# Mixers: the first half's low part of the squares directly behind the second half's mean, and no piece of the weights' conversion in slot 24

## The chip, the cores and the metric

The kernel runs on one core of one Trainium2 chip. The metric is the device time of one execution in microseconds (us), as the median of several runs. Beside it stands one profiled execution, from which all views of the trace come.

## The reference

Three layers follow one another, over 8 batches of 576 positions and 512 channels: a landmark attention, a first mixing layer with an MLP, and a second mixing layer with an MLP. The change lies in the second mixing layer, of which this is the whole:

```python
def _moe2_ref(x, w_ch1, w_ch2):
    X = np.fft.fft(x, axis=1)
    X = np.fft.fft(X, axis=2)
    mixed = np.real(X).astype(np.float32)
    u = x + mixed
    mu = np.mean(u, axis=-1, keepdims=True)
    var = np.mean((u - mu) ** 2, axis=-1, keepdims=True)
    un = (u - mu) / np.sqrt(var + 1e-06)
    ch = np.maximum(un @ w_ch1, 0.0) @ w_ch2
    return (u + ch).astype(np.float32)
```

`w_ch1` is 512 x 2048 and `w_ch2` 2048 x 512, in both MLPs. The results are wanted in single precision.

## The kernel before, in words

**Products.** Every large product is made of three TensorE (PE) matmuls of 128 x 512: each operand is split into a high part, rounded to the matmul's format, and a low part, the rest. The high part is a cast on ScalarE (ACT); the low part, original less high, is a subtraction on VectorE (DVE) or GpSimd (POOL). `split` writes both.

**The stage in question.** From about 650 to 1300 us of the span, PE works through the MLPs in slots (`Mlp.stream`). One slot is 12 matmuls: in the upward half of a chunk one of 8 tiles of hidden units (lines 241 to 243, then `relu` on ACT at line 245 and the low part `g` on DVE at line 246), in the downward half one half of an output tile (lines 294 to 296, and every second slot `xf <- ps + xf` on DVE at line 305, which is then stored by the SP queue at line 153). Three PSUM banks `ps` take turns. After its matmuls a slot runs the steps that a table has put there, and then pieces of other work.

**The mixers.** One `Mixer` per batch does the Fourier transform and the normalization, its steps spread over 31 slots by the table in `steps`. The mixers begin at slots 33, 58, 83, 108, 133, 157, 182 and 206 of the stage; I count them 0 to 7. Slot r of a mixer is r slots behind its begin, so that slots 25 to 31 of one are slots 0 to 6 of the next. The parts that matter here:

- `load` (slot 1): SP issues the transfers of the tile `U` (lines 1169 ff.), of which there is one buffer. `load_first` (slot 3) follows at lines 1178 and 1180. `fold_d` (slots 5 and 7, line 1192) is the first to read it, on DVE.
- `row_high` (slot 5, ACT), `fold_low` (slots 8 and 10, DVE, line 1212) and the transform's matmuls `over_d` (slots 10 to 14, PE, lines 75 to 77, two banks `ps_f`, freed by a `split` into `Z`, line 51).
- `sum_u(n)`, `sums_low(n)` (slots 21 to 23): for half n of the positions the channels of `U` are added (lines 1308 and 1309), cast on ACT (line 1311) and the low part is made on DVE (line 1315; `he` and `ho` for halves 0 and 1).
- `centre(n)` (slot 24 + n): two matmuls with a matrix of ones (line 1320) give the mean, high part first and low part second; DVE takes it from `U` (line 1330, into `Z`).
- `sum_sq(n)` (slot 25 + n): ACT squares (line 1335), DVE adds (lines 1308, 1309), ACT casts (line 1311). `sums_low(n)` again (slot 26 + n, line 1315; now `le` and `lo`).
- `deviation(n)` (slot 28 + n): the same two matmuls (line 1320) on the squares' sums, then the square root on ACT, POOL and DVE.
- `put(n)` (slot 26 + n): SP stores the centred half (line 1355).

**The conversion.** The weights arrive as 64-bit numbers and are converted on the way, in pieces that `Pace.step` hands out at the end of a slot: `room(s)` says how many microseconds of it a slot takes. A tile of weights is four DVE pairs and one split: the pair at lines 1444 and 1445 (called A below), the pair at 1451 and 1453 (B), the pair at 1455 and 1456 (C), and a `split` of which POOL makes the low part. After the 32 tiles, sums of blocks of weights follow (lines 1487 and 1492), each read back from memory by four transfers (line 1477).

Within an engine, and within the SP queue, instructions run in the order in which they were issued.

Of the kernel before, what the change touches and what calls it, by code (L numbers as in the profile page):

```python
# [40 lines left out]
def body(ctx: ExitStack, tc: tile.TileContext, qT, kT, vn, mU, mV, w11, w12, w21, w22,  # L41
# [719 lines left out]
    class Batch:  # L761
# [324 lines left out]
        def steps(self, after):  # L1086

            H0, H1 = slice(0, 512), slice(512, 1152)
            a, b = (2, 1) if self.b > 1 else (0, 0)
            yield from ((2 * (nm == "q") + g - a, lambda nm=nm, g=g: self.landmark(nm, g)) for nm in "kq"  # L1090
                        for g in (0, 1) if (self.b, nm) not in LANDMARKS)
            yield from ((5 - a, self.kernel), (6 - a, self.kernel_norm), (7 - a, self.kernel_t))
            if a:
                yield 6, self.norms
            yield 6, self.scores
            if not a:
                yield 8, self.norms
            yield 9 - b, self.residue
            yield from ((10 - b + i, lambda i=i: self.newton(i)) for i in range(6))
            yield from ( (8, lambda: self.query(0)), (9, lambda: self.query(1)),  # L1100
                        (9, lambda: self.query_exp(H0)), (9, self.scores_sum), (9, lambda: self.query(2)), (10, lambda: self.scores_t(0)),
                        (11, lambda: self.scores_t(1)), (11, self.scores_tail), (11, lambda: self.query_exp(H1)),
                        (11, lambda: self.query_norm(H0)), (12, self.values), (12, lambda: self.query_norm(H1)),
                        (13, lambda: self.query_t(0)), (13, self.query_tail), (14, lambda: self.query_t(1)),
                        (15, self.mixed), (16 - b, self.heads), (17 - b, self.rank))
            if self.b:
                yield 13, lambda: self.mlp.get_tail(self.b)
                yield from ((15 + k // 2, lambda k=k: self.mlp.hand_tail(self.b, k)) for k in range(4))
            yield from ((19 + g, lambda g=g, n=n: self.mix(g, n)) for g in range(2) for n in range(2))
            if after:  # L1110
                yield from ((r, lambda nm=nm: after.load(nm)) for r, nm in ((7, "k"), (10, "q"), (13, "v")))
# [10 lines left out]
    def fourier_setup(f, fc, fp):  # L1122
        q = TAB // 4
        h = fc.tile([P, TAB], F32R, name="tabh")
        l = fc.tile([P, TAB - 148], F32R, name="tabl")
        f["eps"] = fc.tile([P, 1], F32, name="eps")
        nc.gpsimd.memset(f["eps"], 1e-6)
        for i in range(4):
            c = slice(i * q, (i + 1) * q)
            st = fp.tile([P, q], F32, name="big", bufs=2)  # L1130
            nc.sync.dma_start(st, tabs[:, c])
            yield from wait(2)
            n = min(c.stop, TAB - 148) - c.start
            split(h[:, c.start:c.start + n], l[:, c.start:c.start + n], st[:, 0:n], nc.gpsimd if i % 2 else nc.vector)
            if n < q:
                nc.scalar.copy(h[:, c.start + n:c.stop], st[:, n:q])
            yield 1
        f["ones"] = fc.tile([P, P], F32R, name="ones")
        f["row"] = fc.tile([P, NF], F32R, name="row")
        st = fp.tile([P, 1152], F32, name="big", bufs=2)  # L1140
        nc.gpsimd.memset(st[:, 0:S], 0.0)
        yield from wait(2)
        nc.sync.dma_start(zero, st[0:2, 0:S])
        nc.gpsimd.tensor_copy(f["row"], st[:, 0:NF])
        nc.gpsimd.memset(st[:, S:S + P], 1.0 / DM)
        nc.gpsimd.tensor_copy(f["ones"], st[:, S:S + P])
        yield 1
        c = 0
        for nm, n, k in (("cd", 292, 1), ("sd", 292, 1), ("ct", 290, 3), ("sn", 290, 3)):
            f[nm] = [(h[:, c + j * n:c + (j + 1) * n], l[:, c + j * n:c + (j + 1) * n]) for j in range(k)]  # L1150
            c += n * k
        f["alt"] = h[:, c:c + 146]

    class Mixer:
# [205 lines left out]
        def steps(self, last):  # L1360
            e = int(last)
            yield from ((0, self.load_x), (1, self.load), (3, self.load_first), (3, self.fold_x), (4, self.sum_row), (5, self.row_high),
                        (5, lambda: self.fold_d("e")), (5, lambda: self.fold_t("e")), (6, lambda: self.fold_2("e")),
                        (6, self.fold_row), (6, self.row_low), (7, lambda: self.fold_split("e")), (7, lambda: self.fold_d("o")),
                        (8, lambda: self.fold_low("e")), (8, lambda: self.fold_t("o")),
                        (9, lambda: self.fold_2("o")), (9, lambda: self.fold_split("o")),
                        (10, lambda: self.fold_low("o")), (11, self.load_rows))
            yield from ((s, lambda nm=nm, i=i: self.over_d(nm, i)) for s, nm, i in
                        ((10, "e", 0), (11, "e", 1), (12, "e", 2), (13, "o", 0), (14, "o", 1), (14, "o", 2)))
            yield from ((15, self.top_row), (16, lambda: self.odd(0)), (17, lambda: self.even(0)),  # L1370
                        (18, lambda: self.unfold(0)), (18, lambda: self.unfold(3)), (18, lambda: self.odd(1)),
                        (19, lambda: self.even(1)), (20, lambda: self.unfold(1)), (20, lambda: self.unfold(2)),
                        (21, self.store))
            for n in range(2):
                yield from ((21 + n, lambda n=n: self.sum_u(n)), (22 + n, lambda n=n: self.sums_low(n)), (24 + n, lambda n=n: self.centre(n)),
                            (25 + n, lambda n=n: self.sum_sq(n)), (26 + n, lambda n=n: self.sums_low(n)), (28 - e + n, lambda n=n: self.deviation(n)),
                            (26 + n, lambda n=n: self.put(n)), (29 - e + n, lambda n=n: self.newton(n)),
                            (30 - 2 * e + n, lambda n=n: self.put_scale(n)))

# [2 lines left out]
    def pool(name, **k):  # L1382
        return tc.tile_pool(name=name, bufs=1, reuse_waits="tile", **k)

    def chained(gens):
        for g in gens:
            yield from g

    def some(gen, n):
        for _ in range(n):  # L1390
            next(gen, 0)
# [156 lines left out]
    with pool("mm") as mp, pool("pm", space=PSUM) as pm:  # L1548
# [91 lines left out]
        with tc.manual_schedule():  # L1640
            scales = Scales(rs)
            mlp.plan(UN, [(c, c + 1) for c in range(PLAIN, NCH - 2, 2)] + [(NCH - 1, NCH - 2)], quarters)
            with pool("cv") as cv, pool("fp") as fp, pool("fc") as fc, pool("pf", space=PSUM) as psb:
                f = {}
                slots = Slots()
                starts = (33, 58, 83, 108, 133, 157, 182, 206)
                for b, s in enumerate(starts):
                    slots.add(s, Mixer(fp, psb, f, b).steps(b + 1 == B))
                later = Pace(chained([staging_pairs(cv, (2, 3)), staging_sums(cv)]))
                gen = mlp.stream(1)  # L1650
                setup = fourier_setup(f, fc, fp)

                def room(s):
                    r = s - max((a for a in starts if a <= s), default=-99)
                    return 1.45 if r > 40 else 1.4 if r in (*range(10, 21), 23, 24) else .7 if r in (4, 9, 21, 22) else 0

                for s in range(N + 2 * PLAIN * STEPS - LEAD):
                    if s in (N, N + PLAIN * STEPS):
                        some(gen, 9)
                        gen = mlp.stream(2 + (s > N))  # L1660
                    next(gen)
                    slots.run(s)
                    next(setup, 0)
                    later.step(room(s))
                later.rest()
            assert not slots.at
            with pool("tl") as mlp.last_pool, pool("tp", space=PSUM) as mlp.last_ps:
                last = mlp.pairs(quarters, Y, scales, U2, ByChunk(y3), block, block_sums, BLOCKS[-2:])
                next(last)
                for s in range(LEAD):  # L1670
                    next(gen)
                    next(last)
                    next(last)
                some(gen, 9)
                for _ in last:
                    pass
# [83 lines left out]
```

## Time and profile before

| | us |
|---|---|
| median of 3 runs | 1779.37 |
| lowest and highest run | 1777.63, 1780.19 |
| the profiled execution | 1780.39 |
| its span, first to last instruction | 1778.6 |
| PE busy in it | 1747.8 (98%) |
| DVE busy | 1229.9 (69%) |
| ACT busy | 749.2 (42%) |
| POOL busy | 329.6 (19%) |

The granted TensorE clock is full in all 40 slices of the span (mean 0.997). Matmuls overlap: one of 512 columns is recorded with 0.39 us, while the next begins 0.23 us after it. So PE's busy share says little; what counts is where the distance between two matmuls' starts grows. The profiled execution took 1.02 us more than the median.

### The profile page before, as it was taken

How to read it: one execution, taken by the hardware profiler on the slowest of the kernel's cores; microseconds unless marked ns; L12 is line 12 of the kernel's file. 1: busy time of each engine (PE TensorE's matmuls, PEld its weight loads, DVE VectorE, ACT ScalarE, POOL GpSimd, SP SyncE). 2: the span in 40 equal slices, each digit the busy share in tenths (PEclk: the TensorE clock that was granted, in tenths of full speed). 3: DMA queues.
4: the chain of work that ended last, by engine and by line, in shares of the span. 5: the costliest groups of instructions: out<-in, count | busy, mean ns of one | idle time of the engine just before them, and what ended most of it. 6: DMA issues, size and time to landing. Idle time of an engine off the chain costs nothing.

```text
span 1778.6 us, 31053 instructions
## 1 busy us (share of the span) xinstructions
PE 1747.8 (98%) x11869; PEld 1425.3 (80%) x11869; DVE 1229.9 (69%) x2123; ACT 749.2 (42%) x1546; POOL 329.6 (19%) x314
## 2 busy tenths in 40 slices
PE   6999999999999999999999999999999999999998
PEld 4777777777788888888878888888888888888886
DVE  7887666665322977888786665557476887589786
ACT  4544443444211333334332334434256556455543
POOL 3334212221210321211211222211201100100111
PEclk9999999999999999999999999999999999999999
DMA  7555455443536764556464955687488978878974
GB/s 255 178 180 170 153 173 195 171 157 106 180 138 224 254 236 153 177 181 223 160 206 154 346 181 175 228 304 238 157 269 294 326 263 285 260 241 260 327 234 130
DMA packets 224392, 379.92 MB, mean 214 GB/s; under 512 B 29658, under 2 KB 137530, under 8 KB 224244
## 3 DMA queue, kind: packets, MB, share of 16 engines
q1 hardware_dynamic: 218772, 367.72, 61.6%
q10 hardware_dynamic: 5472, 10.23, 1.5%
q8 instruction: 93, 1.52, 0.4%
q14 instruction: 55, 0.45, 0.1%
HBM read 269.00 MB, written 108.27 MB: 212 GB/s over the span
## 4 chain that ended last, share of the span: by engine, by line
PE 87%; DVE 7%; DMA 3%; ACT 1%; issue 1%; SPq 0%; POOL 0%; POOLq 0%; DVEq 0%; ACTq 0%
PE ps L294 9%; PE ps L241 9%; PE ps L296 9%; PE ps L295 9%; PE ps L243 9%; PE ps L242 9%; PE ps L334 8%; PE ps L333 8%; PE ps L332 8%; PE ps_f L76 1%; PE ps_f L77 1%; PE ps_f L75 1%; DMA w<-d 1%; PE ps L803 1%; DMA U<-x 1%
## 5 line engine op out<-in xcount | busy, mean ns | idle before, releaser
L241 PE MATMUL ps<-x,w 128*128 128x512 f32 x768 | 305.5, 398 | 0.2 <-DVE g L246 0.2
L294 PE MATMUL ps<-g,w 128*128 128x512 f32 x768 | 304.1, 396 | 0.0
L243 PE MATMUL ps<-x,w 128*128 128x512 f32 x768 | 299.8, 390 | 0.0
L296 PE MATMUL ps<-g,w 128*128 128x512 f32 x768 | 299.7, 390 | 0.0
L242 PE MATMUL ps<-x,w 128*128 128x512 f32 x768 | 299.5, 390 | 0.0
L295 PE MATMUL ps<-g,w 128*128 128x512 f32 x768 | 299.3, 390 | 0.0
L246 DVE SCALAR_TENSOR_TENSOR g<-ps,g 128x512 fp32r<-128x512 f32 x192 | 132.5, 690 | 206.5 <-ACT g L245 206.0
L245 ACT ACTIVATE g<-ps 128x512 fp32r<-128x512 f32 x192 | 114.2, 597 | 271.3 <-PE ps L243 270.7
L294 PEld LDWEIGHTS ps<-g,w 128*128 128x128 f32 x768 | 144.3, 188 | 32.2 <-issue 3.5
L243 PEld LDWEIGHTS ps<-x,w 128*128 128x128 f32 x768 | 144.1, 188 | 31.3
L296 PEld LDWEIGHTS ps<-g,w 128*128 128x128 f32 x768 | 144.2, 188 | 31.0
L241 PEld LDWEIGHTS ps<-x,w 128*128 128x128 f32 x768 | 144.3, 188 | 30.0 <-DVE g L246 0.6
L295 PEld LDWEIGHTS ps<-g,w 128*128 128x128 f32 x768 | 144.4, 188 | 27.3
L242 PEld LDWEIGHTS ps<-x,w 128*128 128x128 f32 x768 | 144.5, 188 | 27.0
L305 DVE TENSOR_TENSOR xf<-ps,xf 128x512 f32<-128x512 f32 x88 | 60.5, 687 | 92.2 <-PE ps L296 90.1
L414 ACT COPY ps<-ps 128x512 f32<-128x512 f32 x142 | 81.7, 576 | 87.9 <-PE ps L334 81.6
L51 POOL TENSOR_TENSOR stg<-cva,stg 128x512 fp32r<-128x512 f32 x48 | 64.7, 1347 | 216.8 <-ACT stg L50 190.3
L469 POOL TENSOR_TENSOR w<-w,w 128x512 f32<-128x512 f32 x24 | 34.8, 1450 | 363.2 <-DMA w<-rs 207.4
L332 PE MATMUL ps<-xs,w 128*128 128x512 f32 x240 | 93.4, 389 | 0.0
L333 PE MATMUL ps<-xs,w 128*128 128x512 f32 x240 | 93.4, 389 | 0.0
L334 PE MATMUL ps<-xs,w 128*128 128x512 f32 x240 | 93.4, 389 | 0.0
L51 POOL TENSOR_TENSOR x<-xf,x 128x512 fp32r<-128x512 f32 (+7 forms) x48 | 60.9, 1270 | 159.1 <-ACT x L50 123.5
(410 smaller groups left out, 3406.5 us busy)
## 6 DMA issues: line engine op xcount, KB each, us to landing
w<-e SPq DMA_DIRECT2D x96, 512.0 KB
w<-d SPq DMA_DIRECT2D x144, 256.0 KB
wraw<-w SPq DMA_DIRECT2D x56, 512.0 KB
d<-stg SPq DMA_DIRECT2D x48, 512.0 KB
w<-d SPq DMA_DIRECT2D x48, 512.0 KB
y<-xf SPq DMA_DIRECT2D x64, 256.0 KB
xf<-y SPq DMA_DIRECT2D x52, 256.0 KB
u<-u1T ACTq DMA_DIRECT2D x32, 288.0 KB
```

Source lines behind the costliest of these rows:

```text
L51: (eng or nc.vector).tensor_tensor(lo, src, f32(hi), op=ALU.subtract)
L241: nc.tensor.matmul(ps, wh, xh, start=k == 0, stop=False)
L242: nc.tensor.matmul(ps, wl, xh, start=False, stop=False)
L243: nc.tensor.matmul(ps, wh, xl, start=False, stop=k == 3)
L245: nc.scalar.activation(g[:, 0, :], ps, AF.Relu)
L246: nc.vector.scalar_tensor_tensor(out=g[:, 1, :], in0=ps, scalar=0.0, in1=f32(g[:, 0, :]), op0=ALU.max, op1=ALU.subtract)
L294: nc.tensor.matmul(ps, wh, gh, start=k == m0, stop=False)
L295: nc.tensor.matmul(ps, wl, gh, start=False, stop=False)
L296: nc.tensor.matmul(ps, wh, gl, start=False, stop=k == m1 - 1)
L332: nc.tensor.matmul(ps, wh, xh, start=first and k == 0, stop=False, skip_group_check=True)
L333: nc.tensor.matmul(ps, wl, xh, start=False, stop=False, skip_group_check=True)
L334: nc.tensor.matmul(ps, wh, xl, start=False, stop=last and k == 1, skip_group_check=True)
```

## The change

Two edits. In the mixer's table, `sums_low(0)` of the squares moves from slot 26 to slot 25, behind `centre(1)` of the same slot; to get that order the four entries of `centre` and `sum_sq` are taken out of the loop and put ahead of it. `put(0)` thereby stands behind `sum_sq(1)` of its slot instead of ahead of it. In `room`, slot 24 of a mixer gets no conversion work (1.4 us before). Slot 24 exists where the next mixer begins 25 slots later, or never: in mixers 0, 1, 2, 3, 5 and 7.

```diff
@@ -1371,9 +1371,13 @@
                         (19, lambda: self.even(1)), (20, lambda: self.unfold(1)), (20, lambda: self.unfold(2)),
                         (21, self.store))
+            yield 24, lambda: self.centre(0)
+            yield 25, lambda: self.sum_sq(0)
+            yield 25, lambda: self.centre(1)
+            yield 26, lambda: self.sum_sq(1)
             for n in range(2):
-                yield from ((21 + n, lambda n=n: self.sum_u(n)), (22 + n, lambda n=n: self.sums_low(n)), (24 + n, lambda n=n: self.centre(n)),
-                            (25 + n, lambda n=n: self.sum_sq(n)), (26 + n, lambda n=n: self.sums_low(n)), (28 - e + n, lambda n=n: self.deviation(n)),
+                yield from ((21 + n, lambda n=n: self.sum_u(n)), (22 + n, lambda n=n: self.sums_low(n)),
+                            (27 if n else 25, lambda n=n: self.sums_low(n)), (28 - e + n, lambda n=n: self.deviation(n)),
                             (26 + n, lambda n=n: self.put(n)), (29 - e + n, lambda n=n: self.newton(n)),
                             (30 - 2 * e + n, lambda n=n: self.put_scale(n)))
 
@@ -1652,7 +1656,7 @@
-                    return 1.45 if r > 40 else 1.4 if r in (*range(10, 21), 23, 24) else .7 if r in (4, 9, 21, 22) else 0
+                    return 1.45 if r > 40 else 1.4 if r in (*range(10, 21), 23) else .7 if r in (4, 9, 21, 22) else 0
```

Lines of the mixer's functions keep their numbers; the conversion's are 4 higher after the change. Since the conversion hands its pieces out one behind another, leaving out a slot moves every later piece to other slots.

**DVE, mixer 0, slots 23 to 26.** In these rows `Z<-U,ps_l` is `centre`, `cc<-big` and `cc<-cc` are `sum_sq`'s adds, `le` is the low part in question, and `xf<-ps,xf` the output tile that SP stores. Before:

```order
870 L1444 TENSOR_SCALAR cva<-wraw 128x512
871 L1445 SCALAR_TENSOR_TENSOR cva<-wraw,cva 128x512
872 L305 TENSOR_TENSOR xf<-ps,xf 128x512
873 L1330 TENSOR_TENSOR Z<-U,ps_l 128x1152
874 L1451 TENSOR_SCALAR cvp<-cva 128x512
875 L1453 SCALAR_TENSOR_TENSOR cvp<-wraw,cvp 128x512
876 L51 TENSOR_TENSOR x<-xf,x 128x512
877 L1308 TENSOR_TENSOR cc<-big 128x2x288
878 L1309 TENSOR_TENSOR cc<-cc 128x288
879 L1330 TENSOR_TENSOR Z<-U,ps_l 128x1152
880 L305 TENSOR_TENSOR xf<-ps,xf 128x512
881 L1315 TENSOR_TENSOR le<-cc,le 128x288
```

Now, at the same place:

```order
870 L1448 TENSOR_SCALAR cva<-wraw 128x512
871 L1449 SCALAR_TENSOR_TENSOR cva<-wraw,cva 128x512
872 L305 TENSOR_TENSOR xf<-ps,xf 128x512
873 L1330 TENSOR_TENSOR Z<-U,ps_l 128x1152
874 L51 TENSOR_TENSOR x<-xf,x 128x512
875 L1308 TENSOR_TENSOR cc<-big 128x2x288
876 L1309 TENSOR_TENSOR cc<-cc 128x288
877 L1330 TENSOR_TENSOR Z<-U,ps_l 128x1152
878 L1315 TENSOR_TENSOR le<-cc,le 128x288
879 L305 TENSOR_TENSOR xf<-ps,xf 128x512
```

Pair B of slot 24 is gone from here, pair A of slot 23 stays, and `le` and the output tile have changed places.

**DVE, mixer 2, slots 23 to 26.** Before:

```order
1074 L1451 TENSOR_SCALAR cvp<-cva 128x512
1075 L1453 SCALAR_TENSOR_TENSOR cvp<-wraw,cvp 128x512
1076 L1455 TENSOR_TENSOR cvp<-cvp,cva 128x512
1077 L1456 SCALAR_TENSOR_TENSOR cva<-wraw,cvp 128x512
1078 L305 TENSOR_TENSOR xf<-ps,xf 128x512
1079 L1330 TENSOR_TENSOR Z<-U,ps_l 128x1152
1080 L1444 TENSOR_SCALAR cva<-wraw 128x512
1081 L1445 SCALAR_TENSOR_TENSOR cva<-wraw,cva 128x512
1082 L1308 TENSOR_TENSOR cc<-big 128x2x288
1083 L1309 TENSOR_TENSOR cc<-cc 128x288
1084 L1330 TENSOR_TENSOR Z<-U,ps_l 128x1152
1085 L305 TENSOR_TENSOR xf<-ps,xf 128x512
```

Now, behind the same `ho` as the rows above:

```order
1070 L1459 TENSOR_TENSOR cvp<-cvp,cva 128x512
1071 L1460 SCALAR_TENSOR_TENSOR cva<-wraw,cvp 128x512
1072 L305 TENSOR_TENSOR xf<-ps,xf 128x512
1073 L1330 TENSOR_TENSOR Z<-U,ps_l 128x1152
1074 L1308 TENSOR_TENSOR cc<-big 128x2x288
1075 L1309 TENSOR_TENSOR cc<-cc 128x288
1076 L1330 TENSOR_TENSOR Z<-U,ps_l 128x1152
1077 L1315 TENSOR_TENSOR le<-cc,le 128x288
1078 L305 TENSOR_TENSOR xf<-ps,xf 128x512
```

Pair A is gone; pair B has moved to a place ahead of `ho`; `le` is ahead of the output tile.

**DVE, mixer 3, slots 9 to 11.** `Z<-ps_f,Z` frees a bank of the transform. Before:

```order
1112 L1451 TENSOR_SCALAR cvp<-cva 128x512
1113 L1453 SCALAR_TENSOR_TENSOR cvp<-wraw,cvp 128x512
1114 L246 SCALAR_TENSOR_TENSOR g<-ps,g 128x512
1115 L1212 TENSOR_TENSOR lo<-cc,ho 128x578
1116 L51 TENSOR_TENSOR Z<-ps_f,Z 97x2x144
1117 L1455 TENSOR_TENSOR cvp<-cvp,cva 128x512
```

Now:

```order
1106 L246 SCALAR_TENSOR_TENSOR g<-ps,g 128x512
1107 L1212 TENSOR_TENSOR lo<-cc,ho 128x578
1108 L51 TENSOR_TENSOR Z<-ps_f,Z 97x2x144
1109 L1455 TENSOR_SCALAR cvp<-cva 128x512
1110 L1457 SCALAR_TENSOR_TENSOR cvp<-wraw,cvp 128x512
1111 L1459 TENSOR_TENSOR cvp<-cvp,cva 128x512
```

Pair B has moved from ahead of `g` to behind the first `Z`, so that it stands ahead of all later `Z` of this mixer.

## Rows read from the trace of the kernel before

**Rows 1.** Waits of PE over the span: us in total, times, longest us.

```profile
PE ps_l L1320 <- DVE le L1315: 2.5, 2, 1.4
```

**Rows 2.** Timeline of PE, `deviation` of mixer 0: start, duration, what [idle before <- releaser].

```profile
749.77 0.29 PE L1320 MATMUL ps_l<-le,ones 128*128 128x288 f32 x1
751.44 0.40 PE L1320 MATMUL ps_l<-le,ones 128*128 128x288 f32 x1 [1.37 <-DVE le L1315]
...
754.41 0.43 PE L1320 MATMUL ps_l<-lo,ones 128*128 128x288 f32 x2
```

**Rows 3.** Timeline of DVE, mixer 0, slots 23 to 26.

```profile
740.83 1.52 DVE L1444 TENSOR_SCALAR cva<-wraw 128x512 uint32<-128x512 uint32 x1
...
745.83 0.41 DVE L1451 TENSOR_SCALAR cvp<-cva 128x512 uint32<-128x512 uint32 x1
746.27 0.69 DVE L1453 SCALAR_TENSOR_TENSOR cvp<-wraw,cvp 128x512 f32<-128x512 uint32 x1
...
747.49 0.75 DVE L1308 TENSOR_TENSOR cc<-big 128x576 f32<-128x576 f32 x1
...
748.65 1.35 DVE L1330 TENSOR_TENSOR Z<-U,ps_l 128x1152 f32<-128x1152 f32 x1
749.91 0.69 DVE L305 TENSOR_TENSOR xf<-ps,xf 128x512 f32<-128x512 f32 x1
750.51 0.87 DVE L1315 TENSOR_TENSOR le<-cc,le 128x288 fp32r<-128x288 f32 x1
```

**Rows 4.** Timeline of ACT, the same place.

```profile
745.94 1.17 ACT L1335 ACTIVATE big<-Z 128x1152 f32<-128x1152 f32 x1 [0.68 <-DVE Z L1330]
...
749.11 0.61 ACT L50 CAST x<-xf 128x512 fp32r<-128x512 f32 x1
```

**Rows 5.** Timeline of POOL, the same place.

```profile
740.71 1.34 POOL L51 TENSOR_TENSOR stg<-cva,stg 128x512 fp32r<-128x512 f32 x1 [8.66 <-ACT stg L50]
...
749.80 1.27 POOL L51 TENSOR_TENSOR x<-xf,x 128x512 fp32r<-128x512 f32 x1 [6.31 <-ACT x L50]
```

**Rows 6.** Timeline of the SP queue, the same place.

```profile
750.63 0.82 SPq L153 DMA_DIRECT2D x<-xf  x2
...
751.98 1.69 SPq L1169 DMA_DIRECT2D U<-x  x2
```

**Rows 7.** Timelines of DVE and PE, mixer 1, slots 6 to 10.

```profile
761.98 1.36 DVE L1192 TENSOR_TENSOR big<-U 128x1152 f32<-128x1152 f32 x1 [0.99 <-DMA U<-x]
...
767.44 0.69 DVE L246 SCALAR_TENSOR_TENSOR g<-ps,g 128x512 fp32r<-128x512 f32 x1 [1.12 <-ACT g L245]
...
768.31 0.40 PE L241 MATMUL ps<-x,w 128*128 128x512 f32 x1
```

**Rows 8.** Timelines of DVE and PE, from mixer 2's slot 21 to mixer 3's slot 10.

```profile
889.67 0.68 DVE L1455 TENSOR_TENSOR cvp<-cvp,cva 128x512 f32<-128x512 f32 x1
...
898.81 0.69 DVE L51 TENSOR_TENSOR x<-xf,x 128x512 fp32r<-128x512 f32 x1 [1.02 <-ACT x L50]
...
910.07 0.40 PE L1320 MATMUL ps_l<-le,ones 128*128 128x288 f32 x1 [1.13 <-DVE le L1315]
...
921.07 1.36 DVE L1192 TENSOR_TENSOR big<-U 128x1152 f32<-128x1152 f32 x1 [2.76 <-DMA U<-x]
...
927.28 0.50 PE L241 MATMUL ps<-x,w 128*128 128x512 f32 x1 [0.16 <-DVE g L246]
```

**Rows 9.** Timelines of DVE and PE, slot 14 of mixers 3 and 4.

```profile
943.39 0.44 DVE L51 TENSOR_TENSOR Z<-ps_f,Z 97x288 fp32r<-97x288 f32 x1
...
944.04 0.25 PE L75 MATMUL ps_f<-tabl,ho 128*96 128x146 f32 x1
...
1024.05 0.69 DVE L1487 TENSOR_TENSOR wraw<-cva,cvp 128x512 f32<-128x512 f32 x1 [3.26 <-DMA cvp<-d]
...
1026.48 0.36 PE L1267 MATMUL ps_f<-tabh,Z 97*33 97x290 f32 x1 [0.36 <-DVE Z L51]
```

**Rows 10.** One line's instructions, the block sums' reads: duration ns min/median/max, first and last start.

```profile
L1487 DVE TENSOR_TENSOR blk<-cva,cvp x6: 668/678/1180, 994.5 to 1259.5; 128x512 f32<-128x512 f32 x6
```

## The prediction

> **What bounds the kernel now.** I read the waits of PE first, since PE is the engine that is never out of work [rows 1]: over the whole span it waits 2.5 us for `le`, in two places. Then I looked up both places on PE's timeline. In mixer 0, `deviation(0)` begins at 749.77, and its second matmul, the low part's, would follow 0.13 us later (the pair at 754.41 takes 0.43, one matmul alone 0.29 or 0.30). It starts at 751.44 instead [rows 2]: 1.54 us lost, of which the idle entry shows 1.37, since the end of the matmul before covers the rest. In mixer 2 the same matmul starts at 910.07 behind an idle entry of 1.13 [rows 8], so 1.29 lost. The other six mixers show no such wait. Everywhere else in this stage PE begins a matmul every 0.23 us, except for 0.4 us at 927.28 (an idle entry of 0.16, the start 0.55 behind the one before, and the next 0.1 late) and 0.5 us at 1026.48 [rows 8, 9]. So all that this change can give back by PE alone is 1.54 + 1.29 = 2.8 us, and with the two small waits 3.7. About 0.2%, or 3.6 us, is what a measurement of this kernel can tell from no change.
>
> **Edit 1 and edit 2 in mixer 0.** DVE comes to `le` late because it is behind: pair A of slot 23 took 1.52 us for its first half alone [rows 3] while POOL ran [rows 5]. That pair stays. What goes is pair B, 0.41 + 0.69 = 1.1 us, and `le` passes the output tile, 0.6 us (749.91 to 750.51) [rows 3]. Taken alone that is 1.7 us, more than the 1.54 of the wait. But two things behind it are late next.
>
> First, the adds of `sum_sq(0)` cannot start before ACT's square ends, 745.94 + 1.17 = 747.11 [rows 4]; they started at 747.49 [rows 3]. So removing B brings the chain forward by 0.34 us only: adds at 747.15, `centre(1)` at 748.31, `le` at 749.57.
>
> Second, POOL makes a low part `x` from 749.80 for 1.27 us, behind ACT's cast of 749.11 [rows 4, 5], and that cast follows the cast for `le`, so that it too comes 0.34 earlier: POOL from about 749.46 to 750.73. A DVE subtraction from two SBUF tiles that meets a running POOL operation is held: `le` took 0.87 us and ended at 751.38, 0.31 behind POOL's end at 751.07; the first half of pair A ended at 742.35, 0.30 behind POOL's 742.05 [rows 3, 5]. The moved `le` falls 0.11 us behind POOL's new start, is held for almost all of that operation, and ends at 750.73 + 0.31 = 751.04, when PE has wanted it since 749.90. The wait shrinks from 1.54 to about 1.2 us. Bounds: 0.17 (no hold, `le` done at 750.02) and 1.54.
>
> The Trainium skill has a rule on this (SBUF — State Buffer, "Who interferes with whom"): a DVE instruction with two SBUF inputs and a GpSimd instruction that reads SBUF exclude one another for a whole instruction, and the order of issue, not the kind of operation, decides who is blocked. The trace agrees in the two cases above, 0.31 and 0.30 us behind POOL's end; by the rule a `le` that came 0.11 us sooner would not be held at all, and that is the second rival.
>
> **What the output tile drags along.** The tile that `le` passes is waited for by SP: `x<-xf` was issued at 750.63, right behind the tile's end at 750.60, and the loads of `U` for mixer 1 stand behind it in the same queue, at 751.98 [rows 3, 6]. From there a chain runs to PE: DVE waits for `U` and folds it at 761.98; that, a row cast on ACT, `relu` and `g` at 767.44 to 768.13 follow without a gap, and PE needs the bank that this `g` frees at 768.31 [rows 7]. PE's slack there is 0.13 us. Whatever PE gains at 749.90 it therefore loses again at 768, unless `U` comes sooner; and now the tile comes later: `le` to 751.04, the tile to 751.65 instead of 750.60, SP and `U` 1.05 us later, PE at 768.31 - 0.13 + 1.05 = 769.23. Net for mixer 0: **+0.9 us**. Without the hold the tile ends where it did and the net is -0.1; these are the bounds. I take +0.9, since the rows put POOL first, if by little.
>
> **Mixer 2.** Ahead of `le` pair A and the tile (0.6) are gone. I count nothing for A, since `sum_sq(0)`'s adds wait for the square, as in mixer 0. But a pair C (0.68 for a half [rows 8], 1.4 together) no longer stands ahead of this half's first sums, and pair B (1.1) has moved to where DVE waited 1.02 us for a cast of `x` [rows 8], so that it costs nothing there. That makes 0.6 + 1.4 + 1.0 = 3.0 us for `le`, where 1.29 was missing, and 1.4 + 1.0 - 0.45 (`le`, unheld) = 2.0 for the tile and so for `U` of mixer 3, for which DVE waited until 921.07 [rows 8]. The 0.4 at 927.28 is the same chain as at 768; it needs `U` 1.29 + 0.4 = 1.7 sooner, and gets 2.0. So both come back: **-1.7 us**. Bounds: -1.7 and, if the tile comes only 0.4 sooner because a hold takes the rest, -0.4.
>
> **Pieces that move.** Every later piece of the conversion lands elsewhere. In mixer 3 a pair B (1.1 us) now stands ahead of the later `Z`, of which one ended at 943.83 for PE's matmul of 944.04, 0.21 ahead [rows 9]. `g` and the folds ahead of it come sooner once `U` does; I count 0.6 of that, since `relu` still waits for PE. I take **+0.3** for a new wait there (bounds 0 and 1.1 - 0.21 = 0.9). In mixer 4, DVE waited 3.26 us for a block sum's read until 1024.05 and so was late with a `Z` by 0.5 us [rows 9]. In the new order another read stands at the same place, but one sum fewer follows it (0.7): **-0.3** (bounds -0.5 and +0.5, if the read comes as much later as PE comes earlier). The other mixers have no wait to lose; moved pieces there are covered by DVE's idle third. The last conversion pieces slip by a slot or so (2.8 us), and DVE had begun the last read's sum at 1259.5 [rows 10], some 50 us before the stage's end: nothing. `put(0)` keeps its place in SP's order: nothing.
>
> **Sum.** +0.9 - 1.7 + 0.3 - 0.3 = -0.8 us. On the profiled execution's 1780.39 that is 1779.6; the median of the runs was 1779.37, 1.02 below, so I predict 1778.6 us.
>
> **The rivals.**
>
> *The gaps simply close.* The Trainium skill (Perfetto Trace Analysis, "Optimization Strategy") advises to look for gaps on the engine that is to be optimized, and to make what they wait for start sooner. By that way of counting the two waits of `le` are the gain: 2.8 us, 1776.6, and with the small ones 3.7, 1775.7. For it: PE does nothing else but wait there. Against it: the slack of 0.13 at 768 [rows 7], and that `U` is tied to the output tile. It needs `U` to land at least 1.4 us sooner than the SP order suggests. Chance 0.2, half of it beyond 3.6 us.
>
> *No hold in mixer 0.* If `le` gets ahead of POOL, mixer 0 nets -0.1 instead of +0.9, and the sum is -1.8: 1777.6. It hangs on 0.11 us between two starts. Chance 0.28.
>
> *The moved pieces cost more than the waits did.* One mechanism: pair B behind the first `Z` of mixer 3, 0.21 us of slack at 944.04, every microsecond beyond it PE's. If `g` does not come sooner that is 0.9 us, and a hold by POOL on one of its halves (1.52 where the same kind took 0.41 unheld [rows 3], 1.0 or so each) brings 1.9 or, for two, 2.9. With mixer 0's +0.9 and mixer 2's -1.7 the sum is +1.1 to +2.1: 1780.5 to 1781.5. It decides from 0.21 us of delay on. Against it: DVE waits 2.76 us for `U` ahead of that stretch [rows 8], and this wait shrinks. Chance 0.12.
>
> *The change does not do what it says:* had `le` been late for its cast on ACT and not for DVE's backlog, moving it would give nothing. The rows speak against it: it starts directly behind the tile, without idle time of its own [rows 3]. Its time is that of no change, 1779.4. Chance 0.05.
>
> My forecast, -0.8 with a hold in mixer 0 and mixer 2's waits gone, has the remaining 0.35.
>
> **How the numbers follow.** The range takes in the forecast and the rivals up to half of the first one's gain beyond -2.8 us and the third one's lower part, and the runs' own spread of about 1 us: 1776.0 to 1780.9. More than 3.6 us faster: half of the first rival, and a little for the spread, 0.12. More than 3.6 us slower: only the third rival at its worst together with something not seen here, 0.05. No difference that can be told: 0.83.
>
> **What would show it.** Right: in mixers 0 and 2 PE's waits for `le` shrink to about 1.2 us and to nothing; `le` in mixer 0 is recorded with over 1 us and ends about 0.3 behind a POOL `x`; PE has a new wait for `g` (line 246) of over 1 us in mixer 1 near slot 10, and DVE's fold of `U` there starts no earlier against the span than 761.98; the wait at 927.28 is gone. Wrong: no wait of PE at mixer 1's slot 10 (then `U` does not hang on the output tile); `le` of 0.45 us in mixer 0 (no hold); a wait for `Z` of over 1 us in mixer 3 (third rival). If PE's waits fall by over 2.8 us together and the time does not follow, the reading of PE as the bound is wrong.

## The result, and the profile after

| | before | after |
|---|---|---|
| median, us | 1779.85 | 1792.46 |
| runs, lowest and highest | 1777.63 to 1782.35 (6) | 1790.87 to 1795.03 (6) |
| span of the profiled execution | 1778.6 | 1789.1 |

The change makes the kernel 12.6 us slower: ratio 1.007, 95% interval 1.0059 to 1.0080. The forecast was 1778.6 us with a range from 1776.0 to 1780.9; it is wrong in size and in direction. The profiled execution of the changed kernel (1790.87 us) is the fastest of its six, so that the views below account for 10.5 of the 12.6 us; the two slowest runs, 1793.91 and 1795.03 us, have a lower mean granted clock (0.994) than the other four (0.995 to 0.996), and where they lost the time no view shows.

I begin where the prediction began, with PE's waits. In the stage of the mixers they now read (us in total, times, longest us):

```profile
PE ps_f L75 <- DVE Z L51: 3.8, 3, 2.3
PE ps_f L1267 <- DVE Z L51: 2.3, 1, 2.3
PE ps L241 <- DVE g L246: 1.3, 3, 0.5
PE ps L294 <- DVE g L246: 1.1, 1, 1.1
PE ps_l L1320 <- DVE le L1315: 1.0, 1, 1.0
```

The wait for `le`, 2.5 us in two places before [rows 1], is 1.0 in one. In its place stand 6.1 us for `Z` and 2.4 for `g`. `Z` is what frees the bank `ps_f` of the transform, `g` what frees the bank of the MLP's first product.

Where does it happen? From the trace one can take the time at which PE begins each slot, and how much later that is than in the kernel before; I call this the lag. The table says how much of the lag was picked up in each stretch, in us, each from one profiled execution; the first row is the changed kernel, the others are experiments told below.

| kernel | slots 30 to 147, mixers 0 to 3 | 147 to 160, mixer 4 | 160 to 190 | 190 to 206, mixer 6 | 206 to the end, mixer 7 | sum |
|---|---|---|---|---|---|---|
| after | +1.1 | +1.9 | 0.0 | +4.9 | +2.1 | +10.0 |
| edit 2 alone | -0.3 | +2.3 | 0.0 | +4.8 | +2.9 | +9.7 |
| edit 1 alone | +1.6 | 0.0 | 0.0 | -0.2 | +0.4 | +1.7 |
| high parts on POOL | +1.6 | +0.3 | +0.4 | +5.8 | +0.9 | +9.1 |
| room in slot 9 | -0.6 | +1.3 | 0.0 | +5.7 | +2.6 | +9.0 |
| before, sums six slots later | -0.2 | +3.7 | 0.0 | +5.8 | +2.9 | +12.3 |
| after, three slots to the cast | +1.3 | -0.6 | 0.0 | -0.6 | -0.1 | 0.0 |

Mixers 0 to 3, to which nearly the whole prediction was given, lose 1.1 us. Mixers 4, 6 and 7 lose 8.9. One place of mixer 4, from SP's timeline to PE's, in the order of the chain (start, duration, what, [idle before <- releaser]):

```profile
1015.47 1.60 SPq L1510 DMA_DIRECT2D e<-stg  x2
...
1024.95 0.62 ACT L50 CAST stg<-wraw 128x512 fp32r<-128x512 f32 x1 [6.15 <-DMA e<-stg]
1025.47 0.59 ACT L245 ACTIVATE g<-ps 128x512 fp32r<-128x512 f32 x1
1025.96 0.41 ACT L50 CAST Z<-ps_f 97x288 fp32r<-97x288 f32 x1
...
1026.09 0.69 DVE L246 SCALAR_TENSOR_TENSOR g<-ps,g 128x512 fp32r<-128x512 f32 x1 [5.28 <-ACT g L245]
1026.70 0.45 DVE L51 TENSOR_TENSOR Z<-ps_f,Z 97x288 fp32r<-97x288 f32 x1
...
1027.21 0.31 PE L75 MATMUL ps_f<-tabl,ho 128*96 128x146 f32 x1 [2.30 <-DVE Z L51]
```

SP issues the store of a block sum from the buffer `stg` at 1015.47. There is one such buffer. ACT comes to the next cast into it at 1018.80 and stands there until the store has landed, 9.5 us after its issue. Nothing behind the cast on ACT may pass it: not `relu` (line 245), from which DVE makes `g`, and not the cast of `Z`. DVE idles 5.28 us for `relu`, and PE then 2.30 for `Z`.

The same happens at four more casts, two in slots 194 and 195 and two in slots 205 and 206, the second of each pair into `cva`, the one buffer for the high parts of every other sum. ACT and PE:

```profile
1180.76 0.62 ACT L50 CAST stg<-wraw 128x512 fp32r<-128x512 f32 x1 [4.91 <-DMA e<-stg]
...
1185.33 0.62 ACT L50 CAST cva<-blk 128x512 fp32r<-128x512 f32 x1 [3.14 <-DMA e<-cva]
...
1221.09 0.62 ACT L50 CAST stg<-wraw 128x512 fp32r<-128x512 f32 x1 [2.34 <-DMA e<-stg]
1225.03 0.62 ACT L50 CAST cva<-blk 128x512 fp32r<-128x512 f32 x1 [3.32 <-DMA e<-cva]
1225.55 1.16 ACT L1335 ACTIVATE big<-Z 128x1152 f32<-128x1152 f32 x1
...
1183.02 0.31 PE L75 MATMUL ps_f<-tabl,ho 128*96 128x146 f32 x1 [1.06 <-DVE Z L51]
...
1188.87 0.35 PE L1267 MATMUL ps_f<-tabh,Z 97*33 97x290 f32 x1 [2.34 <-DVE Z L51]
```

From the last pair the loss reaches PE by another way. The square of mixer 6's `sum_sq(0)` stands directly behind the held cast (1225.55). Its sums and, behind them on DVE, `centre(1)` come late. `U` is read last by `centre(1)`, so that its load for mixer 7 is issued only at 1229.42, and from there the chain is that of [rows 7]: fold, `relu`, `g`, PE. SP, DVE and PE:

```profile
1229.42 0.89 SPq L1169 DMA_DIRECT2D U<-x  x2
...
1241.68 1.36 DVE L1192 TENSOR_TENSOR big<-U 128x1152 f32<-128x1152 f32 x1 [4.01 <-DMA U<-x]
...
1244.49 0.50 PE L241 MATMUL ps<-x,w 128*128 128x512 f32 x1 [0.50 <-DVE g L246]
...
1248.60 0.50 PE L294 MATMUL ps<-g,w 128*128 128x512 f32 x1 [1.10 <-DVE g L246]
```

The list of ACT's waits sums it up. Neither line exists in the list of the kernel before:

```profile
ACT stg L50 <- DMA e<-stg: 13.4, 3, 6.2
...
ACT cva L50 <- DMA e<-cva: 7.0, 3, 3.3
```

Why not before? There the store of mixer 4 was issued at 1013.15 and the next cast into the buffer came at 1025.50, held by the sum on DVE, and a later one ran without any wait, 7.8 us behind its store of 1198.50; only the one at 1184.62 has an idle entry of 1.55 us, which the trace puts to another transfer. Timeline of ACT, kernel before:

```profile
1025.50 0.62 ACT L50 CAST stg<-wraw 128x512 fp32r<-128x512 f32 x1 [1.71 <-DVE wraw L1492]
...
1206.29 0.62 ACT L50 CAST stg<-wraw 128x512 fp32r<-128x512 f32 x1
```

The planner knows nothing of landing times. `store()` sets `due` to two slots on, some 6.7 us here, and any later slot with room may take the cast. Without the room of slot 24 the pieces shift, and three stores now stand in slots 143, 192 and 203 with the next cast exactly two slots on; before, the casts that follow the stores of these stretches came 7.8 to 12.4 us behind them. Two slots are not too few everywhere: three more stores of the changed kernel, at 1054.02, 1103.86 and 1269.95, have their next cast 6.1, 7.9 and 4.0 us behind them, and none of these casts waits. What marks the two slow stores is what SP had issued ahead of them. In the 13.2 us before each, it issued eleven transfers of the next pass's weights (`w<-d`, line 197), and these stores took 9.5 and 10.7 us; before the store of 1214.94 it issued none for 15 us, and that one took 6.2. Kernel after, SP and the first of the casts that do not wait:

```profile
1054.02 1.56 SPq L1510 DMA_DIRECT2D e<-stg  x2
...
1060.09 0.61 ACT L50 CAST stg<-wraw 128x512 fp32r<-128x512 f32 x1
```

So the theory, **A**: the moved pieces bring ACT's casts of block sums behind stores that have not landed. I call ACT's standing at such a cast a hold. The rivals: **B**, the new order of the steps is to blame (`U` later). **C**, the block sums' reads land late and keep DVE waiting, and not ACT's hold is the loss. **D**, too little room is left for the pieces. **E**, a slot without pieces is itself the loss.

### The profile page after: what moved, and what is told of

The parts are those of the page before. It is cut to its first block, busy times and chain, and to the rows that moved or that the text cites. A ratio compares the mean times of both kernels' runs of the same rounds, so it can differ in the third digit from the quotient of the medians.

```text
span 1789.1 us, 31051 instructions
## 1 busy us (share of the span) xinstructions
PE 1752.6 (98%) x11869; PEld 1427.8 (80%) x11869; DVE 1236.6 (69%) x2123; ACT 748.3 (42%) x1546; POOL 331.5 (19%) x314
## 3 DMA queue, kind: packets, MB, share of 16 engines
q8 instruction: 93, 1.52, 0.4%
```

## The experiments

### Which edit: one of them alone

Edit 2 alone is one line; edit 1 alone is the new table of steps with that line as before.

```diff
-    ... 1.4 if r in (*range(10, 21), 23, 24) else ...
+    ... 1.4 if r in (*range(10, 21), 23) else ...
```

> The kernel before with edit 2 alone: no piece of the conversion in slot 24, the mixers' steps in their old order. Theory A (the pieces that move bring ACT's casts of the block sums behind stores that have not landed, in the stretches in which the next pass's weights are loaded): about 8 to 9.5 us over the kernel before, 1788 to 1789, with waits of ACT for e<-stg and e<-cva of 15 to 20 us in all, PE late in mixers 4, 6 and 7, and a stretch of half clock if one of PE's waits is 2.5 us long. Theory B (the new order of the mixers' steps costs the time, because U is loaded later): within 1.5 us of the kernel before, 1778.5 to 1781.5, and no such waits of ACT.

> The kernel before with edit 1 alone: the new order of the steps, pieces in slot 24 as before. Theory A: 0 to 1.5 us over the kernel before, 1779.9 to 1781.4, no wait of ACT for e<-stg or e<-cva, clock full from start to end. Theory B: 8 to 12 us over it, about 1790, with PE's waits in mixers 4, 6 and 7 as in the changed kernel.

Edit 2 alone: 1789.56 us, ratio 1.0054 (1.0041 to 1.0067), with ACT's waits for the stores of 13.8 and 7.3 us; the time and the waits are a little over what A gave. Edit 1 alone: 1781.17, ratio 1.0005 (0.9996 to 1.0014), with no such wait, and no fall of the clock in this stage. B falls as the cause of the loss; what edit 1 does cost lies in mixer 1, of which more below.

### Neither edit, but the block sums later

```diff
+        for _ in range(6):
+            yield 0
         for n in range(2):
             fetch(n)
```

> The kernel before, neither edit, but the block sums begin six slots later; by the planner's rules their stores then stand in slots 144, 192 and 203 and the next casts from the same buffers two slots behind, as in the changed kernel from mixer 4 on. Theory A (what costs the time is where these stores and casts fall): 7 to 10 us over the kernel before, 1787 to 1790, with ACT's waits for e<-stg and e<-cva of 15 us or more and PE late in mixers 4, 6 and 7. Theory B (the new order of the steps) and theory E (a slot without pieces is itself the loss): within 2 us of the kernel before, 1778 to 1782.

1791.08 us, ratio 1.0062 (1.0049 to 1.0074), as slow as the changed kernel, a little above what A gave. Neither edit is in it, and slot 24 has its pieces. Waits of ACT, and PE's three waits of over 2 us in its timeline, at the places of the changed kernel:

```profile
ACT stg L50 <- DMA e<-stg: 15.9, 3, 7.0
ACT cva L50 <- DMA e<-cva: 7.3, 2, 4.1
```

```profile
1027.05 0.36 PE L1267 MATMUL ps_f<-tabh,Z 97*33 97x290 f32 x1 [2.51 <-DVE Z L51]
...
1183.65 0.31 PE L75 MATMUL ps_f<-tabl,ho 128*96 128x146 f32 x1 [3.20 <-DVE Z L51]
1189.56 0.35 PE L1267 MATMUL ps_f<-tabh,Z 97*33 97x290 f32 x1 [2.37 <-DVE Z L51]
```

B and E fall. What slot 24 has to do with the loss is only that its room decides where the sums fall.

### The changed kernel, with a longer way from store to cast

```diff
             def store():
                 ...
-                due[nm] = clock[0] + 2
+                due[nm] = clock[0] + 3
```

> The changed kernel, but the planner lets a cast into a sum's buffer follow the store from it after three slots (some 11 us) instead of two. Theory A: ACT's waits for e<-stg and e<-cva shrink from 20 us to under 4, PE's delays in mixers 4, 6 and 7 fall from 9.4 us to under 3, the clock stays full; the last sums now run past this stage's end, which may cost 0 to 4 us there: 1783 to 1788. Theory C (the reads land late): the delays stay, since the reads stay among the weights' transfers, 1790 to 1796. Theory D (too little room left): slower still than the changed kernel, by the two sums that run past the end, 1793 to 1800.

1782.41 us, ratio 1.0014 (1.0005 to 1.0022): one slot more between store and cast gives back 10 of the 12.6 us. The lag of PE in mixers 4, 6 and 7 is gone altogether (table), and the clock stays full. ACT's waits:

```profile
ACT stg L50 <- DMA e<-stg: 2.6, 1, 2.6
...
ACT cva L50 <- DMA e<-cva: 0.2, 1, 0.2
```

The hold of 2.6 us that is left (mixer 4, the cast of 1022.74) costs PE nothing: the lag does not grow there. POOL waits 8.7 us for a store in mixer 6, and PE loses nothing by that either. This speaks for A and against D. Against C it speaks less, since the longer way moves the reads too; the next experiment is the better test of C. The plain way to take the wait away, a second buffer, was not tried.

### The hold moved from ACT to POOL

```diff
-            split(hi, lo, out, nc.gpsimd)
+            nc.gpsimd.tensor_copy(hi, out)
+            nc.gpsimd.tensor_tensor(lo, out, f32(hi), op=ALU.subtract)
```

> The changed kernel, every piece in its place, but the block sums' high parts are cast on POOL instead of ACT, so that POOL and not ACT stands behind a store that has not landed. Theory A: ACT's waits for e<-stg and e<-cva are gone, relu (line 245) and the casts of Z come in time, and 6 to 9 us come back, 1783.5 to 1786.5, less what POOL's own low parts of x and Z lose behind the same stores (not more than 2 us, as the sums' low parts stood behind the cast before). Theory C (it is not the hold but the block sums' reads, which land late among the weights' transfers and keep DVE waiting): the time stays within 2 us of the changed kernel, 1790.5 to 1794.5. Theory D (there is simply too little room left for the pieces): the same, 1790.5 to 1794.5.

1787.50 us, ratio 1.0044 (1.0030 to 1.0057), between the two forecasts. ACT's waits for the stores are gone, and with them nearly all of mixer 4's loss and half of mixer 7's, as A says; C and D had 1790.5 or more. Mixer 6 loses more than in the changed kernel. Timelines of POOL, DVE and PE there:

```profile
1179.56 0.61 POOL L1506 CAST stg<-wraw 128x512 fp32r<-128x512 f32 x1 [10.79 <-DMA e<-stg]
...
1185.32 1.72 DVE L1491 TENSOR_TENSOR wraw<-wraw 128x512 f32<-128x512 f32 x1 [6.46 <-POOL cva L1506]
1186.96 0.68 DVE L246 SCALAR_TENSOR_TENSOR g<-ps,g 128x512 fp32r<-128x512 f32 x1
1187.56 0.81 DVE L51 TENSOR_TENSOR Z<-ps_f,Z 96x288 fp32r<-96x288 f32 x2
...
1188.06 0.46 PE L1267 MATMUL ps_f<-tabh,Z 97*33 97x290 f32 x1 [3.87 <-DVE Z L51]
```

POOL now stands behind the store, DVE's next sum waits, by the trace for POOL's cast, and `g` and `Z` stand behind that sum. Of mixer 6's 5.8 us, 1.7 are lost in the slot behind this wait, at a granted clock of 0.5. My allowance of 2 us for POOL had left out that DVE waits for POOL in turn. So the hold costs the time wherever it is put; the engine decides by which way it reaches PE.

### The room given back elsewhere

```diff
-    ... else .7 if r in (4, 9, 21, 22) else 0
+    ... else 2.1 if r == 9 else .7 if r in (4, 21, 22) else 0
```

> The changed kernel with slot 24's room (1.4 us) given to slot 9 of each mixer, where 0.7 stood. By the planner's rules the block sums' pieces of mixers 4 and 5 then stand nearly where they stood before the change (the first sum's store in slot 132, the next cast from the same buffer in slot 138), and those from mixer 6 on where they stand in the changed kernel (store in slot 192, cast in 194). Theory A: PE's delay of about 2 us in mixer 4 is gone, those of mixers 6 and 7 (7.4 us with the half clock) stay: 1789.5 to 1791.5, with ACT's waits for stores in mixers 6 and 7 alone. Theory D (too little room): all of it comes back, 1779.5 to 1782. Theory B (the new order): as the changed kernel, 1791 to 1794.

1788.65 us, ratio 1.0052 (1.0039 to 1.0064), a little under A's range. Mixers 6 and 7 lose 5.7 and 2.6, with ACT's waits for stores at four casts and only there; so D falls, since the room is all there. But mixer 4, where I expected nothing, still loses 1.3 us, with no hold of ACT. Timelines of DVE and PE:

```profile
1023.85 0.69 DVE L1491 TENSOR_TENSOR wraw<-cva,cvp 128x512 f32<-128x512 f32 x1 [4.56 <-DMA cvp<-d]
...
1025.79 0.81 DVE L51 TENSOR_TENSOR Z<-ps_f,Z 96x288 fp32r<-96x288 f32 x2
...
1026.29 0.35 PE L1267 MATMUL ps_f<-tabh,Z 97*33 97x290 f32 x1 [1.67 <-DVE Z L51]
```

That is C, and it is what the kernel before has at the same place with 3.26 us [rows 9]. C exists, then, as the same thing on another engine: DVE stands at a sum whose read has not landed. It is not what cost mixers 6 and 7.

### The sums in their old places

Slot 24 is left free in mixers 0 to 2 alone, and slots 21 and 22 there get 1.4 each; every block sum has its slot of the kernel before. Once with the new order of steps, once with the old one.

```diff
+    if r in (21, 22, 24) and s < 108:
+        return 0 if r == 24 else 1.4
     return 1.45 if r > 40 else 1.4 if r in (*range(10, 21), 23, 24) else ...
```

> The changed kernel's order of steps in all mixers, but slot 24 is left free in mixers 0 to 2 alone, and its room is given to slots 21 and 22 there; every block sum then has its slot of the kernel before. Theory A: mixers 0 to 3 cost what they did in the changed kernel (its PE was 0 to 1.1 us behind there), mixers 4, 6 and 7 lose nothing, no wait of ACT for a block sum's store: 1779.5 to 1781.5. Theory B: about 1789 to 1792. Theory E (a slot without pieces is itself the loss): 3 of 7 mixers, 1784 to 1786.

> As the kernel with slot 24 free in mixers 0 to 2 alone, but with the mixers' steps in their old order. Theory A: PE's path through mixers 0 to 3 as in the kernel with edit 2 alone, which was 0.3 us ahead of the kernel before from slot 24 of mixer 0 to the end of mixer 3, and nothing lost behind it: 1778.5 to 1780.5, no difference from the kernel before that can be told, or faster by up to 1.3 us. Theory E: 1784 to 1786.

1784.44 us (1.0022, 1.0013 to 1.0031) and 1783.24 (1.0015, 1.0007 to 1.0024): 3 us over what I expected of each. From mixer 4 to the end PE picks up 0.1 and 0.4 us in sum, with no wait of ACT for a sum's store, as A says and B does not. The 3 us are a side effect of the test. They lie in mixers 0 and 2 (2.5 us, with some 1.5 more behind it at a granted clock of 0.5, and over 1 us), where the pieces that I had put into slots 21 and 22 made `ho` late; mixer 0, DVE, then PE (new order):

```profile
741.91 1.51 DVE L1315 TENSOR_TENSOR ho<-cc,ho 128x288 fp32r<-128x288 f32 x1
...
743.48 0.40 PE L1320 MATMUL ps_l<-ho,ones 128*128 128x288 f32 x1 [2.24 <-DVE ho L1315]
```

By their totals alone these two come near E, which gave 1784 to 1786. The wait decides: it is for `ho`, behind the pieces added to slots 21 and 22, and not behind an empty slot 24. The kernels with three slots to the cast, where slot 24 is empty in all six mixers that have one (E's estimate had counted seven), lose nothing in mixers 4, 6 and 7.

### The step on the output tile

The kernel with three slots to the cast, in which `le` of the first half goes back behind the output tile. Its new slot, 26, also has the second half's two adds ahead of it, so that in mixer 0 `le` changes places with the tile and with these adds.

```diff
-    (27 if n else 25, lambda n=n: self.sums_low(n))
+    (27 if n else 26, lambda n=n: self.sums_low(n))
```

> The changed kernel with three slots between store and cast, and in every mixer but for one pair of rows on DVE the same: le of the first half again stands behind the output tile (slot 26). It tests the step of the prediction on mixer 0 and 1: le held back the tile, the tile held SP's x<-xf and with it the load of U, and PE lost 1.2 us in slots 67 and 68. By that theory DVE's fold of U and g of mixer 1 come some 1 us sooner, PE's losses at these two slots fall from 1.24 us to under 0.4, PE's wait for le in mixer 0 stays between 0.9 and 1.3; the time is 0.5 to 1.5 us under the same kernel with le ahead of the tile, 1781 to 1782. Rival: U is late for the steps' order ahead of it (centre and the squares), not for the tile; then the losses at slots 67 and 68 stay over 1 us and the time does not move.

1785.50 us, 1.0032 (1.0021 to 1.0044): 3 us slower where I expected it faster. The half that the prediction spoke of is right. With `le` ahead of the tile SP issues `U`'s load at 751.87 and DVE folds at 761.84; with the tile first, SP and DVE:

```profile
750.83 1.71 SPq L1169 DMA_DIRECT2D U<-x  x2
...
760.90 1.35 DVE L1192 TENSOR_TENSOR big<-U 128x1152 f32<-128x1152 f32 x1
```

Both come 0.9 to 1.0 us sooner: the tile does hold `U`. PE's losses at slots 67 and 68 (0.56 and 0.68 us) are gone too, but that shows little, since PE itself was 2.7 us later by then. For the second half's adds now stand ahead of `le` as well, and PE's wait in mixer 0 grows to 2.48 us instead of 1.06, with a stretch of low clock behind it. In the last mixer PE waits for `le` anew, 1.32 us, and loses 1.6; that is half of the 3 us. PE in mixer 0:

```profile
751.76 0.40 PE L1320 MATMUL ps_l<-le,ones 128*128 128x288 f32 x1 [2.48 <-DVE le L1315]
```

The two ends of the chain cannot both be had by this exchange.

### Edit 2 without its hold, and a control

> Edit 2 alone (no piece in slot 24, old order of steps) with three slots between store and cast. If the holds were all that edit 2 costs, and its gain at le in mixers 0 and 2 (0.34 + 1.4 + 0.3 us of PE's path, less 1.8 of small losses in mixers 1 to 3) is kept, then PE is 0 to 1.4 us ahead of the kernel before at the stage's end: 1778.5 to 1782. If edit 2 costs something else, 1784 or more.

> The kernel before, neither edit, with three slots between store and cast. A control: it has no wait of ACT for a block sum's store, so that the longer distance takes no wait away; the sums end later, as they do with it in the changed kernel. Theory A: 1779.5 to 1782, as far from the kernel before as the sums' later end costs. If it is 3 us faster or more, the distance does something else than theory A says.

Edit 2 alone with three slots: 1781.15 us, 1.0010 (1.0001 to 1.0019). The kernel before with three slots: 1780.79, 1.0005 (0.9996 to 1.0013); the longer way gives nothing where there was no hold. The control has one short hold of its own, 2.2 us for `e<-cva` at 1182.55, by which PE loses nothing. In the first, ACT's holds are down to 2.9 us in all; PE gains 1.6 us on the kernel before up to the stage's end and loses it again at the seam to the last stage, for the last sums now run past the end. PE's waits from 1290 to 1380 us; the kernel before has none from 1300 us on:

```profile
PE ps L334 <- DMA xf<-d: 0.8, 1, 0.8
PE ps L332 <- ACT ps L414: 0.4, 1, 0.4
```

> Edit 2 alone with three slots between store and cast for the first 15 stores of block sums and two for the rest: every piece stands where it stands in the same kernel with three slots throughout, but the last four sums are stored in slots 231 and 232 instead of 237 and 238, ahead of the stage's end. There PE was 1.6 us ahead of the kernel before at the stage's end (from slot 30 on, by the profiles) and lost 1.8 us at the seam to the last stage. If the late sums cause the loss at the seam, it falls under 0.5 us and the kernel is 0.5 to 1.7 us faster than the kernel before, 1778.6 to 1779.9 against 1780.3; if the seam costs the same, 1780.5 to 1781.5.

```diff
-                due[nm] = clock[0] + 3
+                due[nm] = clock[0] + (3 if stores else 2)
+                stores.pop() if stores else None
 ...
-        later = []
+        later, stores = [], [0] * 15
```

1779.32 us beside 1779.83, ratio 0.9998 (0.9989 to 1.0007). The loss at the seam is gone, but a new wait of 0.8 us for `le` in the last mixer, 1.2 us of PE's path, took much of what was won. It is the best of the kernels run, and not to be told from the kernel before.

## Why the prediction was wrong

**The waits of PE in mixer 0: right.** The prediction left 1.2 of 1.54 us. `le` is held by POOL, ends 0.31 us behind it, and PE's wait entry falls from 1.37 to 1.04. DVE, POOL, SP and PE after:

```profile
750.55 1.48 DVE L1315 TENSOR_TENSOR le<-cc,le 128x288 fp32r<-128x288 f32 x1
...
750.44 1.28 POOL L51 TENSOR_TENSOR x<-xf,x 128x512 fp32r<-128x512 f32 x1 [5.96 <-ACT x L50]
...
754.01 1.69 SPq L1169 DMA_DIRECT2D U<-x  x2
...
752.09 0.40 PE L1320 MATMUL ps_l<-le,ones 128*128 128x288 f32 x1 [1.04 <-DVE le L1315]
766.78 0.50 PE L241 MATMUL ps<-x,w 128*128 128x512 f32 x1 [0.36 <-DVE g L246]
770.18 0.50 PE L241 MATMUL ps<-x,w 128*128 128x512 f32 x1 [0.39 <-DVE g L246]
```

`le` began 0.11 us behind POOL's `x`, the margin that the prediction had worked out, and took 1.48 us; the same operation took 0.45 unheld, at 1229.31. The trace agrees with the Trainium skill's rule (SBUF — State Buffer, "Who interferes with whom") that a DVE instruction with two SBUF inputs contends with a GpSimd instruction that reads SBUF, and that the order of issue decides who is blocked. Of the two cases that the prediction gave for this rule only `le` is one: the first half of pair A was held as well (1.52 us where most of its kind take 0.42), but it reads one SBUF tile, `wraw`.

**The output tile and `U`: right in kind.** The changed execution is 1.0 us late before mixer 0's slot 24 already, so that `U`'s load at 754.01 instead of 751.98 is 1.0 us late by the change, as predicted. Predicted 0.9 net for mixer 0; PE gained 0.34 at `le` and lost 1.7 in slots 67 to 73, +1.3 together. The one wait of over 1 us for `g` that was named as a sign did not come: there are two, of 0.36 and 0.39, with 1.2 us lost by them. The exchange of tile and `le` shows that the tile holds `U`. "No hold", "the gaps simply close" and "the change does nothing" are out for this part of the kernel.

**Mixers 2 and 3: right in kind, short in size.** The wait in mixer 2 went, 1.8 us of PE's path for 1.7 predicted; mixer 3's `Z` cost 0.6 for 0.3. Two small losses, 0.45 in slot 94 and 0.42 in slot 109, were not foreseen; PE's second matmul of a group starts late there for a low part of DVE. From mixer 0 to 3 this makes +1.1 for the -0.5 predicted.

**The step that failed** is "Pieces that move", in two sentences: mixer 4's "-0.3 (bounds -0.5 and +0.5)" and "the other mixers have no wait to lose; moved pieces there are covered by DVE's idle third". Measured: +1.9 in mixer 4, +4.9 in 6 and +2.1 in 7. The -0.3 itself was right in kind: mixer 4 gains 0.6 where three slots take the hold away, and in the changed kernel too PE gets 0.6 back one slot behind the 2.5 us that the hold costs. In mixer 6, 0.5 came back that was not foreseen, a late start for `le` of line 1212 at 1164.49 (idle entry 0.31), which the prediction's reading of PE had missed. What was missing is the hold. I priced the moved pieces by the engine on which most of their time lies, DVE, and looked there for slack. A piece of the block sums also has a cast on ACT and a store on SP, and the cast needs a buffer that the store before must have left. That is a wait that the trace of before does not show, and it should have had bounds: zero, and a store's landing less the time until ACT comes to the cast. That time is not the planner's two slots: at 1015.47 it was 3.3 us, and 9.5 less 3.3 is the hold of 6.15. The rows to suspect it from were there: ACT's wait for `d<-stg`, the same pattern in the weights' pieces, 17.3 us in 8 places and up to 4.2 long in the kernel before. But those lie between 607 and 666 us, and PE lost nothing there, so that these rows alone did not give a price.

The third rival, "the moved pieces cost more than the waits did", said the right thing in general but had the wrong place and mechanism (mixer 3's `Z`) and came to +1.1 to +2.1 us; "more than 3.6 us slower" had 0.05.

**The clock.** 1.6 us of mixer 6's loss are not waits. Windows of the changed kernel around 1190 (columns: PE, PEld, DVE, ACT and POOL busy us with their instructions, granted clock, DMA share, GB/s):

```profile
1180.00:1190.10 10.10, 6.70 (x39) 5.28 (x38) 4.76 (x7) 3.79 (x9) 2.55 (x2) 1.00 0.92 306
1190.20:1193.50 3.30, 3.30 (x9) 2.64 (x8) 0.45 (x1) 0.12 (x1) 0.00 (x0) 0.50 0.99 311
1193.70:1200.00 6.30, 6.30 (x37) 5.59 (x36) 3.07 (x6) 2.62 (x5) 0.57 (x1) 1.00 0.56 180
```

PE was busy for 6.7 of 10.1 us; then the granted clock stood at 0.50, the lower level of 1.2 GHz, for 3.4 us, and PE began 9 matmuls where full clock makes some 14. The prediction priced a wait of PE at its own length.

**What stays open.** The kernel with three slots to the cast is still 2.2 us above the kernel before by the medians; by its profile 1.4 us of that are the seam, the rest is within the spread of the runs. Why two of the stores took so long is not shown. The DMA share does not tell them apart: between issue and release it was 0.97 and 1.00 for the slow ones and 1.02 for the one of 6.2 us. That they stood behind the weights' transfers fits the rows, but no run took these away.

## What to carry to other kernels

When pieces of background work move, follow every instruction of a piece on its own engine, and for each ask which buffer it writes and whose transfer must have left it; a cast behind an unlanded store holds all that stands behind it in that engine's order. A table that spaces such pieces should count from the landing that the trace shows at its slowest place, not from a number of slots that happened to do. An edit that takes room from such a table is an edit of everything behind it: compare what lies between each store and the next use of its buffer, over the whole stage.

## What the runs showed of the hardware

- A store of two 256 KB transfers from SP took 9.5 and 10.7 us until its buffer was free where SP had issued eleven weights' transfers in the 13.2 us ahead of it, 6.2 us at 1214.94 behind none, and at most 4.0 us at 1269.95, also behind none. The Trainium skill (DMA: Bandwidth & Descriptors, "Anatomy of one DMA — SWDGE (gpsimd) path") gives for one transfer of another kind, issued by GpSimd, 2.0 us and the bytes at 436 GB/s, an estimate of 3.2 us for the two; by such a price two slots would have been ample. The stores at which ACT waited took about two to over three times that.
- Behind waits of PE of 2.2 to 3.9 us the granted clock fell to 0.5 in eight of the kernels, for 3.4 us in six and 6.8 in two, and PE lost 1.4 to 2.3 us more in the slot behind. But it did not fall behind each such wait: the changed kernel kept the full clock behind 2.30 us in mixer 4, and with the sums six slots later PE waited 3.20 and 2.37 us in mixer 6 and kept it too. Which of these waits costs the clock I could not have said beforehand.
